# A decode kernel on one core: half of the last row of `wo` loaded early through three DMA engines, and exp on pairs of tiles

## The chip, the cores and the metric

The kernel runs on one core of a Trainium2 chip. The metric is the device time of one execution in microseconds (us), here the median of three to nine runs. The core has a tensor engine (PE, with a separate row PEld for its weight loads), a vector engine (DVE), a scalar engine (ACT), GpSimd (POOL), a sync engine (SP, which here only issues loads) and 16 DMA engines that move data from HBM into the on-chip memory (SBUF, 128 partitions).

## The reference, cut to what matters

One token passes through attention against a cache of 65,536 keys and values (32 query heads, 4 key/value heads), and through a gated MLP; a gate mixes the two.

```python
def _A_ref(x, k_cache, v_cache, wq, wo):        # x 1x1x1024, caches 1x4x65536x128, bf16
    q = (x @ wq) ...                            # wq 1024 x 4096
    scores = jnp.einsum('bhqd,bhkd->bhqk', q, k) * Dh ** (-0.5)
    p = _softmax(scores, axis=-1)
    o = jnp.einsum('bhqk,bhkd->bhqd', p, v)
    return o.reshape(B, Sq, Hq * Dh) @ wo       # wo 4096 x 1024
...
return g * a + (1 - g) * b                      # b: the MLP with w_in and w_out
```

The caches are 134 MB of the 162 MB that must be read. `wo` is the last thing needed, 8 MB.

## The kernel before: the parts that matter here

Everything large passes through one tile, `kv`, of five slots of 32 KB per partition. One function issues every load from the sync engine's queue.

```python
WO_SPLIT = ((16,), (8, 4, 2, 1, 1))
...
    const = ctx.enter_context(tc.tile_pool(name="const", bufs=1))
    wk = ctx.enter_context(tc.tile_pool(name="wk", bufs=2))
    big = ctx.enter_context(tc.tile_pool(name="big", bufs=1))     # kv lies behind const and wk
    scp = ctx.enter_context(tc.tile_pool(name="scp", bufs=NT + 1))
    ptp = ctx.enter_context(tc.tile_pool(name="ptp", bufs=NT + 2))
...
    kv = big.tile([P, NKV * CT * P], BF16, name="kv")
    def load(src, shape, at):
        ...
        v = kv[:, int(at * CT * P):int(at * CT * P) + n]
        ins = nc.sync.dma_start(out=v, in_=src)
```

Softmax works tile by tile, four tiles for each of the four key/value heads:

```python
        for j in range(NT):
            nc.scalar.activation(out=sct[g, j][:], in_=sct[g, j][:], func=ACT.Exp, scale=SCALE,
                                 bias=nb[:, 0:1], accum_out=lss[g][:, j:j + 1])
            ptt[g, j] = ptp.tile([P, CC, B], BF16, name="pt")
            nc.vector.transpose(out=ptt[g, j][:].rearrange("p c x -> p (c x)"),
                                in_=sct[g, j][:])
```

At the end, partition p holds rows 32p to 32p+31 of `wo`, and they arrive in pieces of 16, 8, 4, 2, 1 and 1 rows per partition, each multiplied as it comes. The pieces get smaller so that little work is left after the last one.

```python
    wo_view = A_wo.rearrange("(p c) n -> p c n", c=OC)            # OC = 32
    c0 = 0
    for at, split in enumerate(WO_SPLIT):
        for n in split:
            t = load(wo_view[:, c0:c0 + n, :], (n, D), at + c0 % (OC // 2) * D / (CT * P))
            project(t, n, oa, c0, last=(c0 + n == OC))
            c0 += n
    ...
    nc.scalar.copy(out=out_sb[:], in_=out_ps[:])                  # then two 1 KB output DMAs
```

## Time and profile before

| | before |
|---|---|
| time, median (lowest to highest) | 383.25 us (383.17 to 383.29) |
| span of the profile | 381.4 us |
| DMA engines busy, queue 1 | 98.7% of 16 engines' span |
| read from HBM | 162.01 MB, 425 GB/s over the span |
| PE, DVE, ACT busy | 61%, 57%, 10% |

The first lines are from the page: busy us and share of the span by engine; the DMA's busy tenths in 40 equal slices; then the DMA queues with packets, MB and share of 16 engines' time. Queue 1 carries the loads, queues 8 and 14 carry instructions for the engines themselves.

```profile
PE 232.4 (61%) x1372; PEld 56.8 (15%) x796; DVE 218.4 (57%) x211; ACT 39.6 (10%) x55; POOL 4.4 (1%) x10
...
DMA  9999999999999999999999999999999999999995
...
q1 hardware_dynamic: 4324, 162.01, 98.7%
q8 instruction: 8, 0.13, 0.1%
q14 instruction: 3, 0.02, 0.0%
```

The DMA engines are the limit: they are full in all slices but the last. What can be gained without moving fewer bytes is what lies in that last slice. The windows view shows it: each row is a stretch of time, and its last two columns are the DMA engines' busy share and GB/s.

```profile
core 0: us, PE busy (x) PEld busy (x) DVE busy (x) ACT busy (x) POOL busy (x), PEclk, DMA share, GB/s
371.20:376.00 4.80, 3.79 (x85) 2.87 (x77) 0.00 (x0) 0.00 (x0) 0.00 (x0) 0.70 0.98 398
376.00:377.00 1.00, 0.62 (x16) 0.42 (x16) 0.00 (x0) 0.00 (x0) 0.00 (x0) 1.00 0.83 322
377.00:378.00 1.00, 0.40 (x8) 0.28 (x8) 0.00 (x0) 0.00 (x0) 0.00 (x0) 0.75 0.58 215
378.00:379.00 1.00, 0.69 (x12) 0.19 (x7) 0.00 (x0) 0.00 (x0) 0.00 (x0) 0.50 0.08 29
```

The share falls in steps over 2 us, so the 16 engines do not finish together, though each has the same bytes to move. The timeline of the same end, and the softmax of one head group (start us, us, engine, line, operation, and in brackets the idle time before and what ended it):

```profile
377.60 1.08 PE L478 MATMUL out_ps<-kv,oa 128*32 128x256 bf16 x12 [0.64 <-DMA kv<-in_A_wo_dram]
378.92 0.41 PE L478 MATMUL out_ps<-kv,oa 128*32 128x256 bf16 x4 [0.24 <-DMA kv<-in_A_wo_dram]
379.37 0.37 ACT L521 CAST out_sb<-out_ps 128x256 bf16<-128x256 f32 x1 [45.36 <-PE out_ps L478]
379.77 0.32 SPq L524 DMA_DIRECT2D out_dram<-out_sb  x1
```

```profile
252.14 0.16 DVE L420 TENSOR_SCALAR nb<-nb_ps 128x1 f32<-128x1 f32 x1 [0.53 <-PE nb_ps L417]
253.66 4.64 DVE L427 STREAM_TRANSPOSE pt<-sc 128x1024 bf16<-128x1024 bf16 x4 [1.37 <-ACT sc L424]
...
275.76 0.33 SPq L167 DMA_DIRECT2D kv<-in_A_k_cache_dram  x1
```

The last matmuls wait for the last piece of `wo`, so the kernel ends when the slowest DMA engine ends. The load that SP issues at 275.76 joins a queue that is not empty: the load ahead of it finished at 279.1 to 281.1 on the 16 engines.

**Following single DMA engines.** The trace holds the start, length, size and queue of every DMA packet, though not its engine. An engine takes its next packet 3 or 4 ns before the previous record ends, so packets can be chained into 16 lanes, one for each engine (where two lanes coincide to the nanosecond their names can be swapped; ends and packet lengths are not affected). In the kernel before, seven lanes write their last completion at 376.31 to 377.09 us of the span and nine at 377.89 to 378.37. The late ones are those that an instruction fetch fell on: eight 16,384-byte packets of queue 8, one on each of eight engines, each of which sets its engine back by 1.55 us for the rest of the run, and two 8,192-byte packets of queue 14 that fell on a ninth. The third packet of queue 14, at 318 us, fell on one of the seven early lanes and sets it back by about 0.7 us; it is the one that ends at 377.09.

### The profile page before, as it was taken

What the parts mean: (1) busy time and instruction counts of PE and PEld (TensorE: products, weight loads), DVE (VectorE), ACT (ScalarE), POOL (GpSimd) and SP (SyncE); (2) the same over time, 40 slices, a digit from 0 to 9 for tenths busy, and PEclk for the clock granted to TensorE, in tenths of its full rate; (3) what the DMA queues carried; (4) which work ended last, traced back from release to release, by engine and by line L of the source; (5) the groups of instructions that cost most, each with busy time, mean ns of one, the idle gap of its engine ahead of it and who ended that gap; (6) DMA issues with size and microseconds to landing.
All of it is one profiled execution on the core that took longest, in us unless ns stands there. A gap on an engine that the chain in (4) does not pass through costs nothing.

```text
span 381.4 us, 2581 instructions
## 1 busy us (share of the span) xinstructions
PE 232.4 (61%) x1372; PEld 56.8 (15%) x796; DVE 218.4 (57%) x211; ACT 39.6 (10%) x55; POOL 4.4 (1%) x10
## 2 busy tenths in 40 slices
PE   0433467678157944796397629872967196849355
PEld 0110011112011210121011101120111011212123
DVE  4241487996687506966977059669780488550040
ACT  1010001111601100114010001050001010500000
POOL 4000000000000000000000000000000000000000
PEclk9966659998759895989588959895799679969766
DMA  9999999999999999999999999999999999999995
GB/s 376 439 426 416 433 436 440 436 461 429 400 426 440 440 435 426 440 440 440 440 428 440 440 440 433 428 427 406 433 440 428 426 433 427 440 411 436 440 405 230
DMA packets 4375, 162.17 MB, mean 425 GB/s; under 512 B 520, under 2 KB 524, under 8 KB 908
## 3 DMA queue, kind: packets, MB, share of 16 engines
q1 hardware_dynamic: 4324, 162.01, 98.7%
q8 instruction: 8, 0.13, 0.1%
q14 instruction: 3, 0.02, 0.0%
q10 hardware_dynamic: 40, 0.01, 0.0%
HBM read 162.01 MB, written 0.00 MB: 425 GB/s over the span
## 4 chain that ended last, share of the span: by engine, by line
DMA 59%; PE 20%; DVE 16%; issue 2%; ACT 1%; SPq 1%; DVEq 0%; ACTq 0%
DMA kv<-in_A_k_cache_dram 37%; PE s_ps L391 15%; DVE kv L384 9%; DMA kv<-in_A_wo_dram 8%; DMA kv<-in_A_wq_dram 7%; DMA kv<-in_A_v_cache_dram 7%; PE o_ps L437 3%; DVE pt L427 2%; DVE mx L386 1%; DVE o_sb L451 1%; PE q_ps L277 1%; ACT sc L424 1%; DVE rowt L447 1%; ACT sc L402 1%; SPq L167 1%
## 5 line engine op out<-in xcount | busy, mean ns | idle before, releaser
L391 PE MATMUL s_ps<-kv,wt 128*128 128x512 bf16 x512 | 142.1, 437 | 81.8 <-DVE kv L384 81.7
L384 DVE STREAM_TRANSPOSE kv<-kv 128x2048 int32<-128x2048 int32 x64 | 142.7, 2280 | 55.5 <-DMA kv<-in_A_k_cache_dram 55.5
L437 PE MATMUL o_ps<-kv,pt 128*64 128x512 bf16 x512 | 61.6, 399 | 7.7 <-DMA kv<-in_A_v_cache_dram 7.7
L391 PEld LDWEIGHTS <-wt 128*128 128x128 bf16 x256 | 27.5, 108 | 197.6 <-issue 140.2
L402 ACT CAST sc<-s_ps 128x1024 bf16<-128x1024 f32 x16 | 16.2, 1013 | 253.5 <-PE s_ps L391 253.5
L437 PEld LDWEIGHTS <-pt 128*64 128x64 bf16 x256 | 16.0, 115 | 50.7 <-issue 48.1
L427 DVE STREAM_TRANSPOSE pt<-sc 128x1024 bf16<-128x1024 bf16 x16 | 18.6, 1217 | 6.8 <-ACT sc L424 6.8
L386 DVE TENSOR_REDUCE mx<-sc 128x1 f32<-128x1024 bf16 x12 | 14.5, 1207 | 10.1 <-ACT sc L402 10.1
L424 ACT ACTIVATE sc<-sc,nb 128x1024 bf16<-128x1024 bf16 x16 | 18.2, 1137 | 12.2 <-DVE nb L420 12.2
L447 DVE TENSOR_TENSOR rowt<-o_ps,own 128x1024 f32<-128x1024 f32 x4 | 4.8, 1194 | 24.9 <-PE o_ps L437 24.9
L457 PE MATMUL om_ps<-o_sb,hsel 128*32 128x128 f32 x8 | 2.5, 421 | 19.7 <-DVE o_sb L451 19.7
L406 DVE TENSOR_REDUCE mx<-sc 128x1 f32<-128x1024 bf16 x4 | 4.9, 1220 | 14.2 <-ACT sc L402 14.2
L277 PE MATMUL q_ps<-kv,xT 128*32 128x512 bf16 x64 | 7.2, 627 | 7.4 <-DMA kv<-in_A_wq_dram 7.4
L478 PE MATMUL out_ps<-kv,oa 128*32 128x256 bf16 x128 | 6.7, 366 | 3.7 <-DMA kv<-in_A_wo_dram 2.2
L277 PE MATMUL z_ps<-kv,xT 128*32 128x448 bf16 x64 | 6.2, 570 | 3.8 <-DMA kv<-in_B_w_in_dram 3.8
L344 DVE TENSOR_TENSOR rowt<-q_ps,own_b 128x512 f32<-128x512 f32 x2 | 1.3, 686 | 12.5 <-PE q_ps L277 12.5
L451 DVE TENSOR_REDUCE o_sb<-rowt 128x128 f32<-128x1024 f32 x4 | 7.5, 1872 | 0.1
L292 DVE TENSOR_TENSOR rowt<-z_ps,own_b 128x448 f32<-128x448 f32 x2 | 1.2, 620 | 8.5 <-PE z_ps L277 8.5
L233 PE MATMUL xb_ps<-xg,spread 8*128 8x256 bf16 x1 | 0.4, 367 | 9.1 <-DMA xg<-in_gate_w_dram 9.1
L277 PEld LDWEIGHTS <-xT 128*32 128x32 bf16 x64 | 3.0, 139 | 19.4 <-issue 19.3
L478 PEld LDWEIGHTS <-oa 128*32 128x32 bf16 x128 | 4.4, 124 | 6.1 <-issue 3.3
L521 ACT CAST out_sb<-out_ps 128x256 bf16<-128x256 f32 x1 | 0.4, 372 | 45.4 <-PE out_ps L478 45.4
(88 smaller groups left out, 54.8 us busy)
## 6 DMA issues: line engine op xcount, KB each, us to landing
kv<-in_A_k_cache_dram SPq DMA_DIRECT2D x4, 4096.0 KB, 26.8
kv<-in_A_wq_dram SPq DMA_DIRECT2D x2, 4096.0 KB, 32.8
kv<-in_A_v_cache_dram SPq DMA_DIRECT2D x2, 4096.0 KB
kv<-in_B_w_in_dram SPq DMA_DIRECT2D x2, 3584.0 KB, 15.0
kv<-in_A_wo_dram SPq DMA_DIRECT2D x1, 4096.0 KB
kv<-in_B_w_out_dram SPq DMA_DIRECT2D x1, 3584.0 KB
kv<-in_A_wo_dram SPq DMA_DIRECT2D x1, 2048.0 KB, 28.6
kv<-in_A_wo_dram SPq DMA_DIRECT2D x1, 1024.0 KB, 30.7
```

The lines of the kernel that those rows point to most:

```text
L277: ins = nc.tensor.matmul(ps[t * B:(t + 1) * B, k * HN:k * HN + n], lhsT=xT[:, i * KH + c:i * KH + c + 1].to_broadcast([P, B]), rhs=w[:, c, ...
L384: nc.vector.transpose(out=kb[:, v * n:(v + 1) * n], in_=kb[:, v * n:(v + 1) * n])
L386: nc.vector.reduce_max(**late.pop())
L391: ins = nc.tensor.matmul(s_ps[:, k * HN:(k + 1) * HN], lhsT=wt[g % 2][:, v, b].rearrange("p a v h -> p (a v h)"), rhs=kx[:, b // 2, b % 2, ...
L402: nc.scalar.copy(out=sct[g, j][:], in_=s_ps[:])
L406: nc.vector.reduce_max(**late.pop())
L424: nc.scalar.activation(out=sct[g, j][:], in_=sct[g, j][:], func=ACT.Exp, scale=SCALE, bias=nb[:, 0:1], accum_out=lss[g][:, j:j + 1])
L427: nc.vector.transpose(out=ptt[g, j][:].rearrange("p c x -> p (c x)"), in_=sct[g, j][:])
L437: ins = nc.tensor.matmul(o_ps[g][hs, e, :], lhsT=ptt[g, j][:, 2 * u:2 * u + 2, :].rearrange("p c x -> p (c x)"), rhs=vx[:, 2 * u + e], sta ...
L447: nc.vector.tensor_tensor(out=om8, in0=o_ps[g][:].rearrange("p e (v d) -> p (e v) d", d=DH), in1=own_8[:].unsqueeze(2).to_broadcast([P, 2 ...
L451: nc.vector.tensor_reduce(out=o_sb[:], in_=om8.rearrange("p x d -> p d x"), axis=AX.X, op=ALU.add)
L478: nc.tensor.matmul(out_ps[t * B:(t + 1) * B, :], lhsT=vec[:, c0 + c:c0 + c + 1].to_broadcast([P, B]), rhs=w[:, c, t * NO:(t + 1) * NO], st ...
```

## The change

Its intent is to even out that end. The last row of each partition is 256 KB. For the 64 even partitions it is still loaded last, by all 16 engines. For the 64 odd ones it is loaded early, between the loads of the caches, in seven small loads of nine rows and one of one row. Each of the seven has an outer dimension of 3 and is meant for three engines that finish early. The rows land in a tile `moved` on partitions 0 to 23, three rows each, and a one-hot matmul brings the matching attention outputs there. To make room in SBUF, exp and the transposes that follow run on pairs of tiles with fewer buffers. Eight dummy matmuls, two groups of 1.04 us in the trace, keep PE busy around the last head's output.

```diff
-WO_SPLIT = ((16,), (8, 4, 2, 1, 1))
+WO_SPLIT = ((16,), (8, 4, 2, 1))
+MA, MB, MM = 3, 8, 3
-    scp = ctx.enter_context(tc.tile_pool(name="scp", bufs=NT + 1))
-    ptp = ctx.enter_context(tc.tile_pool(name="ptp", bufs=NT + 2))
+    scp = ctx.enter_context(tc.tile_pool(name="scp", bufs=NT // 2))
+    ptp = ctx.enter_context(tc.tile_pool(name="ptp", bufs=NT // 2 + 1))
+    moved = const.tile([MA * MB, MM, D], BF16, name="moved")
+    src_row = const.tile([P, MM, MA, MB], FP32, name="src_row")
... (one-hot tables; some small tiles go from double to single buffers)
-        for j in range(NT):
-            nc.scalar.activation(out=sct[g, j][:], in_=sct[g, j][:], func=ACT.Exp, scale=SCALE,
-                                 bias=nb[:, 0:1], accum_out=lss[g][:, j:j + 1])
+        for h in range(NT // 2):
+            sc = sct[g, h][:].rearrange("p t x -> p (t x)")
+            nc.scalar.activation(out=sc, in_=sc, func=ACT.Exp, scale=SCALE,
+                                 bias=nb[:, 0:1], accum_out=lss[g][:, h:h + 1])
+            ptt[g, h] = ptp.tile([P, 2 * CC, B], BF16, name="pt")
+            nc.vector.transpose(out=ptt[g, h][:].rearrange("p c x -> p (c x)"), in_=sc)
...
+    last_odd = wo_view[1::2, OC - 1, :]
+    def load_moved(b):
+        r0, na, nm = b * MA * MM, MA, MM          # the eighth load: one row
+        ...
+        nc.sync.dma_start(
+            out=moved[b:b + (na - 1) * MB + 1:MB, :nm, :],
+            in_=last_odd[r0:r0 + na * nm, :].rearrange("(a m) d -> a m d", m=nm))
...
             vn = load_kv(A_v_cache, g - 1, 2 * h, 3, 2)
+            load_moved(2 * g - 2 + h)
...
+    keep_busy(4)
     head_out(G - 1)
+    keep_busy(4)
...
+    t = kv[:, c0 * D:(c0 + 1) * D]
+    nc.sync.dma_start(out=t[0::2, :], in_=wo_view[0::2, c0, :])
+    project(t.unsqueeze(1), 1, oa_kept, 0, last=True)
```

The new tiles stand in the pool ahead of `kv`, so `kv` moves from byte 28128 of each partition to byte 30784.

More of the change, by code (lines that the diff above doesn't have):

```diff
@@ L64 @@
     assert S % (P * CT) == 0 and F == 2 * NB * ZN and ZN == B * FC and HD == NHB * NB * HN
-    assert NHB * NB == 2 * G and CC * B == 2 * HN and sum(map(sum, WO_SPLIT)) == OC
+    assert NHB * NB == 2 * G and CC * B == 2 * HN and sum(map(sum, WO_SPLIT)) == OC - 1
     const = ctx.enter_context(tc.tile_pool(name="const", bufs=1))
@@ L203 @@
     nc.gpsimd.memset(ones_f[:], 1.0)
+    moved = const.tile([MA * MB, MM, D], BF16, name="moved")
+    nc.gpsimd.memset(moved[:], 0.0)
+    src_row = const.tile([P, MM, MA, MB], FP32, name="src_row")
+    nc.gpsimd.iota(src_row[:], pattern=[[2, MM], [2 * MM, MA], [2 * MM * MA, MB]], base=1,
+                   channel_multiplier=0, allow_small_or_imprecise_dtypes=True)
     wt = [big.tile([P, VC, BP, NB, VC, REP], BF16, name=f"wt{i}") for i in range(2)]
@@ L206 @@
         nc.gpsimd.memset(t[:], 0.0)
-    pbits = const.tile([P, 6], I32, name="pbits")
+    pbits = const.tile([P, 7], I32, name="pbits")
     for i, m in enumerate((P // KC - 1, B - 1, QD - 1, REP - 1)):
@@ L215 @@
                             scalar2=2 * VC - 1, op0=ALU.logical_shift_right, op1=ALU.bitwise_and)
-    pf = const.tile([P, 7], FP32, name="pf")
+    nc.vector.tensor_scalar(out=pbits[:, 6:7], in0=pidx[:], scalar1=1, scalar2=None,
+                            op0=ALU.bitwise_and)
+    pf = const.tile([P, 8], FP32, name="pf")
     nc.vector.tensor_copy(out=pf[:, 0:1], in_=pidx[:])
-    nc.vector.tensor_copy(out=pf[:, 1:7], in_=pbits[:])
+    nc.vector.tensor_copy(out=pf[:, 1:8], in_=pbits[:])
     def one_hot(shape, dtype, in0, col, name):
@@ L234 @@
                      start=True, stop=True)
-    xm = const.tile([P, 2, KC, P // KC], FP32, name="xm")
+    rowt = big.tile([P, 2 * HN], FP32, name="rowt")
+    xm = rowt[:, :2 * P].rearrange("p (t c i) -> p t c i", t=2, c=KC)
     for t in range(2):
@@ L240 @@
     xa = const.tile([P, 2, KC], FP32, name="xa")
-    nc.vector.tensor_reduce(out=xa[:], in_=xm[:], axis=AX.X, op=ALU.add)
+    nc.vector.tensor_reduce(out=xa[:], in_=xm, axis=AX.X, op=ALU.add)
     xT = const.tile([P, KC], BF16, name="xT")
@@ L267 @@
     own_q = one_hot([P, QD], FP32, row[:, :QD], 3, "own_q")
+    move = one_hot([P, MM * MA * MB], BF16, src_row[:].rearrange("p m a b -> p (m a b)"), 0, "move")
+    keep = const.tile([P, 1], BF16, name="keep")
+    nc.vector.tensor_scalar(out=keep[:], in0=pf[:, 7:8], scalar1=-1.0, scalar2=1.0, op0=ALU.mult,
+                            op1=ALU.add)
     hsel = one_hot([P, REP, QD], FP32, row[:, :REP].unsqueeze(2).to_broadcast([P, REP, QD]), 4,
@@ L287 @@
         x_rows(z_ps, win_t[i], ZN, i)
-    rowt = big.tile([P, 2 * HN], FP32, name="rowt")
     om8 = rowt[:].rearrange("p (x d) -> p x d", d=DH)
@@ L400, in k_tile @@
             mxs[g] = wk.tile([P, NT], FP32, name="mx")
-        sct[g, j] = scp.tile([P, CC * B], BF16, name="sc")
-        nc.scalar.copy(out=sct[g, j][:], in_=s_ps[:])
-        late.append(dict(out=mxs[g][:, j:j + 1], in_=sct[g, j][:], axis=AX.X))
+        if (g, j // 2) not in sct:
+            sct[g, j // 2] = scp.tile([P, 2, CC * B], BF16, name="sc")
+        sc = sct[g, j // 2][:, j % 2]
+        nc.scalar.copy(out=sc, in_=s_ps[:])
+        late.append(dict(out=mxs[g][:, j:j + 1], in_=sc, axis=AX.X))
     def stats(g):
@@ L413, in stats @@
                                 axis=AX.X, op=ALU.max)
-        gr = wk.tile([1, P // REP, REP], FP32, name="gr")
+        gr = big.tile([1, P // REP, REP], FP32, name="gr")
         nc.vector.tensor_copy(out=gr[:], in_=gm[:].unsqueeze(1).to_broadcast([1, P // REP, REP]))
@@ L421, in stats @@
                                 op0=ALU.mult)
-        lss[g] = wk.tile([P, NT], FP32, name="ls")
-        for j in range(NT):
-            nc.scalar.activation(out=sct[g, j][:], in_=sct[g, j][:], func=ACT.Exp, scale=SCALE,
-                                 bias=nb[:, 0:1], accum_out=lss[g][:, j:j + 1])
-            ptt[g, j] = ptp.tile([P, CC, B], BF16, name="pt")
-            nc.vector.transpose(out=ptt[g, j][:].rearrange("p c x -> p (c x)"),
-                                in_=sct[g, j][:])
+        lss[g] = wk.tile([P, NT // 2], FP32, name="ls")
+        for h in range(NT // 2):
[4 more added lines that the diff above has]
+            nc.vector.transpose(out=ptt[g, h][:].rearrange("p c x -> p (c x)"), in_=sc)
     def v_tile(g, j, vt):
@@ L435, in v_tile @@
             hs = slice(u % 2 * P // 2, (u % 2 + 1) * P // 2)
+            c0 = j % 2 * CC + 2 * u
             for e in range(2):
@@ L438, in v_tile @@
                     o_ps[g][hs, e, :],
-                    lhsT=ptt[g, j][:, 2 * u:2 * u + 2, :].rearrange("p c x -> p (c x)"),
+                    lhsT=ptt[g, j // 2][:, c0:c0 + 2, :].rearrange("p c x -> p (c x)"),
                     rhs=vx[:, 2 * u + e], start=(j == 0 and u < 2),
@@ L449, in head_out @@
             in1=own_8[:].unsqueeze(2).to_broadcast([P, 2 * VC, DH]), op=ALU.mult)
-        o_sb = wk.tile([P, DH], FP32, name="o_sb")
+        o_sb = big.tile([P, DH], FP32, name="o_sb")
         nc.vector.tensor_reduce(out=o_sb[:], in_=om8.rearrange("p x d -> p d x"), axis=AX.X,
                                 op=ALU.add)
-        om_ps = psm.tile([P, DH + NT], FP32, name="om_ps", tag="m")
+        om_ps = psm.tile([P, DH + NT // 2], FP32, name="om_ps", tag="m")
         hs = hsel[:].rearrange("p h q -> p (h q)")
@@ L461, in head_out @@
         nc.vector.reciprocal(out=rl[gs, 1:2], in_=rl[gs, 0:1])
-        om = wk.tile([P, QD, OC], FP32, name="om")
+        om = big.tile([P, QD, OC], FP32, name="om")
         nc.vector.tensor_tensor(
@@ L470, in head_out, with keep_busy @@
                                 scalar2=gate[gs, :], op0=ALU.mult, op1=ALU.mult)
+    def keep_busy(n):
+        ps = pss.tile([P, 2 * HN], FP32, name="busy_ps", tag="s")
+        w = wt[G % 2][:].rearrange("p v b t u h -> p (v b t u h)")
+        for i in range(n):
+            ins = nc.tensor.matmul(ps[:, :HN], lhsT=w[:, :P], rhs=w[:, :HN], start=True,
+                                   stop=True, skip_group_check=True)
+            if i > 0:
+                same_weights(ins)
     NO = D // NB
@@ L479, in project @@
                     out_ps[t * B:(t + 1) * B, :],
-                    lhsT=vec[:, c0 + c:c0 + c + 1].to_broadcast([P, B]),
+                    lhsT=vec[:, c0 + c:c0 + c + 1].to_broadcast([vec.shape[0], B]),
                     rhs=w[:, c, t * NO:(t + 1) * NO],
@@ L483, in project @@
                     skip_group_check=True)
+    wo_view = A_wo.rearrange("(p c) n -> p c n", c=OC)
+    last_odd = wo_view[1::2, OC - 1, :]
+    def load_moved(b):
+        r0, na, nm = b * MA * MM, MA, MM
+        if r0 + MA * MM > P // 2:
+            assert r0 == P // 2 - 1
+            na, nm = 1, 1
+        nc.sync.dma_start(
+            out=moved[b:b + (na - 1) * MB + 1:MB, :nm, :],
+            in_=last_odd[r0:r0 + na * nm, :].rearrange("(a m) d -> a m d", m=nm))
     build_w(0)
@@ L506 @@
     for j, n, at in ((0, 2, 1), (2, 1, 3), (3, 1, 4)):
-        for i, vt in enumerate(load_kv(A_v_cache, G - 1, j, at, n)):
+        vn = load_kv(A_v_cache, G - 1, j, at, n)
+        if j < 3:
+            load_moved(MB - 2 + j // 2)
+        for i, vt in enumerate(vn):
             v_tile(G - 1, j + i, vt)
+    keep_busy(4)
     head_out(G - 1)
-    wo_view = A_wo.rearrange("(p c) n -> p c n", c=OC)
+    keep_busy(4)
     c0 = 0
@@ L516 @@
             t = load(wo_view[:, c0:c0 + n, :], (n, D), at + c0 % (OC // 2) * D / (CT * P))
-            project(t, n, oa, c0, last=(c0 + n == OC))
+            project(t, n, oa, c0)
             c0 += n
+            if c0 == OC // 2:
+                mv_ps = psm.tile([MA * MB, MM], FP32, name="mv_ps", tag="m")
+                for m in range(MM):
+                    nc.tensor.matmul(mv_ps[:, m:m + 1],
+                                     lhsT=move[:, m * MA * MB:(m + 1) * MA * MB],
+                                     rhs=oa[:, OC - 1:OC], start=True, stop=True,
+                                     skip_group_check=True)
+                oa_moved = wk.tile([MA * MB, MM], BF16, name="oa_moved")
+                nc.vector.tensor_copy(out=oa_moved[:], in_=mv_ps[:])
+                oa_kept = wk.tile([P, 1], BF16, name="oa_kept")
+                nc.vector.tensor_tensor(out=oa_kept[:], in0=keep[:], in1=oa[:, OC - 1:OC],
+                                        op=ALU.mult)
+            if c0 == OC - OC // 4:
+                project(moved, MM, oa_moved, 0)
+    t = kv[:, c0 * D:(c0 + 1) * D]
+    nc.sync.dma_start(out=t[0::2, :], in_=wo_view[0::2, c0, :])
+    project(t.unsqueeze(1), 1, oa_kept, 0, last=True)
     out_sb = const.tile([P, NO], BF16, name="out_sb")
```

## The prediction

> **What bounds the kernel.** The 16 DMA engines. In the 40-slice view DMA is 9 tenths in 39 slices; queue 1 fills 98.7% of 16 engines' span, 162.01 MB at 425 GB/s. PE (61%) and DVE (57%) hide beneath it. Loads are issued 4 us or more before the previous load's last packet has landed (sync engine's timeline beside the packets' completion writes), so the engines do not run dry. In the windows at the end the DMA share falls 0.98, 0.83, 0.58, 0.08 (371-376, then each us to 379): the engines do not finish together. Following each engine's packets in the trace, seven end 1.2 to 2.1 us before the last one, nine within 0.5 us of it. The late ones are those that once served a 16,384-byte packet of the instruction queue (eight, 1.02 to 1.10 us each), which puts that engine's later completions back 1.55 us for good. [...]
>
> **What the change does.** The bytes stay. The last row per partition (256 KB, eight 2,048-byte packets per engine, 84 ns each, one every 81 ns) becomes four packets per engine: 4 x 81 ns = 0.32 us less on every engine. The other 64 rows go early to few engines[...]. Each gets 21 rows, 21 x 81 ns = 1.7 us (estimate). So the change pays if those three are early ones: they would end level with the late ones (-1.9 + 1.7). [...]
>
> Moved besides:
> - exp on pairs: first exp about 2.1 us in place of 1.14, so the transposes of pt end about 0.8 us later per head group, and loads are issued up to 0.8 us later; the 4 us lead covers that. It mainly makes room for `moved`.
> - eight busy matmuls (0.4 us each) around the last head's output, while PE waits anyway (3.1 and 1.4 us).
> - twelve matmuls for `moved` (0.6 us) before the 4-column piece, whose data comes at 376.3; the first 24 columns were done at 375.0. Off the path.
> - a few tiny operations and eight small DMA issues, about 0.4 us each of an idle sequencer.
>
> **On the path:** only the end of the wo stream: last landing 378.9 to about 378.6; then the same tail (matmuls 0.43, cast 0.37, output DMA).
>
> **Prediction:** 383.22 - 0.3 = 382.95 us, 8 in 10 between 382.6 and 383.8. Faster by over 2% 0.005, within 2% 0.985, slower by over 2% 0.01.
>
> **What would show it right:** the last project begins about 0.3 us earlier; the spread of the engines' last packets is smaller; loads still lead, slices still 9; transposes of pt about 0.8 us later per group; instruction refills still eight.
>
> **What would make it wrong:** if one of the three engines has served a refill, it ends 1.7 - 0.3 = 1.4 us after the end of before: about 384.6 us. If refills fall on other engines from run to run, the times scatter by that. If 2 KB packets between K and V cost more than 81 ns, part of the gain goes. If the late exp makes loads late, a slice under 9 shows it. If `moved`'s matmuls delay the last pieces, the gain is given back there.

383.22 us less about 0.3 us for the shorter end of the stream gives the 382.95 us (382.92 by the rounded figures). "Those three" are the three engines that I took an outer dimension of 3 to use. No trace of the kernel before showed it; that of the changed kernel has the early rows on three lanes.

## More of the kernel before

Each of the three groups of experiments ran on another chip, with the kernel before beside it (medians 383.28, 383.25 and 383.20 us), so times of different groups can be compared to about 0.1 us.

## The result, and the profile after

| | before | after |
|---|---|---|
| time, median (lowest to highest), 5 runs | 383.25 us (383.17 to 383.29) | 383.58 us (383.50 to 383.88) |
| span of the profile | 381.4 us | 381.6 us |
| last completion write of the loads, us of the span | 378.37 | 378.60 |
| time minus span | 1.8 to 1.9 us | 1.9 to 2.4 us |

The ratio of after to before is 1.0012, with a 95% interval from 0.9998 to 1.0025. A ratio here is the mean time of one kernel's runs over that of the other's of the same rounds, so it is not quite the ratio of the medians quoted. The interval is about 1 us wide in all, which is more than most effects; so the verdicts below rest on the traces, and on the spans of all runs, as much as on the times.

The same views of the changed kernel: the page's lines, the windows of the end, the timeline of the end, and the softmax of the same head group with the same load.

```profile
PE 229.6 (60%) x1395; PEld 56.0 (15%) x813; DVE 221.1 (58%) x208; ACT 37.3 (10%) x39; POOL 7.2 (2%) x12
...
DMA  9999999999999999999999999999999999999995
...
q1 hardware_dynamic: 4346, 162.01, 98.8%
q8 instruction: 8, 0.13, 0.1%
q14 instruction: 2, 0.02, 0.0%
```

```profile
371.20:376.00 4.80, 3.47 (x111) 2.94 (x112) 0.32 (x3) 0.00 (x0) 0.00 (x0) 1.00 0.97 399
376.00:377.00 1.00, 0.02 (x4) 0.02 (x7) 0.00 (x0) 0.00 (x0) 0.00 (x0) 1.00 0.87 342
377.00:378.00 1.00, 0.60 (x16) 0.40 (x16) 0.00 (x0) 0.00 (x0) 0.00 (x0) 1.00 0.72 277
378.00:379.00 1.00, 0.54 (x12) 0.30 (x12) 0.00 (x0) 0.00 (x0) 0.00 (x0) 1.00 0.11 39
```

```profile
378.86 0.29 PE L502 MATMUL out_ps<-kv,oa 128*32 128x256 bf16 x4 [0.22 <-DMA kv<-in_A_wo_dram]
379.15 0.41 PE L502 MATMUL out_ps<-kv,oa_kept 128*32 128x256 bf16 x4
379.60 0.37 ACT L579 CAST out_sb<-out_ps 128x256 bf16<-128x256 f32 x1 [45.65 <-PE out_ps L502]
380.00 0.28 SPq L582 DMA_DIRECT2D out_dram<-out_sb  x1
```

```profile
251.07 0.16 DVE L434 TENSOR_SCALAR nb<-nb_ps 128x1 f32<-128x1 f32 x1 [0.53 <-PE nb_ps L431]
253.45 4.50 DVE L442 STREAM_TRANSPOSE pt<-sc 128x2048 bf16<-128x2048 bf16 x2 [2.22 <-ACT sc L439]
...
274.68 0.34 SPq L168 DMA_DIRECT2D kv<-in_A_k_cache_dram  x1
```

The end is more even than before (0.72 in place of 0.58 in the third row of the windows), as intended, but the whole of it comes later: the last project begins at 379.15 and not at 378.92. The pairs of exp act as predicted: from `nb` to the end of the transposes of `pt` it takes 253.45 + 4.50 - 251.07 = 6.9 us, against 253.66 + 4.64 - 252.14 = 6.2 us before. No load is late for it: SP issues the same load at 274.68, even earlier than before, while the load ahead of it ends at 279.0 to 281.2, and from 12 us to the `wo` pieces no engine pauses for over 0.1 us but at instruction fetches.

The chains of packets show that three points of the plan work. The nine rows of an early load lie on three lanes, three each, so the load does run on three engines. These three lanes serve no instruction fetch. And the half row shortens the end of every lane: from the last completion but one to the last it takes 0.67 us on the earliest lane before, 0.34 us after.

But the chains also show packets that have grown. In the kernel before, a packet of 65,536 bytes takes 2,419 to 2,428 ns, and only those beside an instruction fetch take more. Here is what the changed kernel's trace has around the sixth early load (start in ns of the span, length in ns, bytes, cut to the packets over 9 ns):

```
317501 2698 65536
317770 2536 65536
...
319197   84  2048
319204   84  2048
319272 2533 65536
319274 2532 65536
319277   84  2048
...
319451 2614 65536
319564 2532 65536
319650 2689 65536
319679 2532 65536
319715 2571 65536
```

Here every lane's packet that is in flight just after the early load takes some 110 ns more, and a few take 250 ns more. This happens at early loads 4, 5 and 6 (counted from 0), with most packets longer by some 80 ns at load 4, 110 at load 5 and 130 at load 6, where they have 32,768 bytes. At loads 0 to 3 only one to three lanes are hit.

### The profile page after: what moved, and what is told of

It reads as the page before. It is cut to its first block, busy times and chain, and to the rows that moved or that the text cites. A ratio compares the mean times of both kernels' runs of the same rounds, so it can differ in the third digit from the quotient of the medians. Undisturbed runs are those within 1.5% of the kernel's fastest.

```text
span 381.6 us, 2611 instructions
## 1 busy us (share of the span) xinstructions
PE 229.6 (60%) x1395; PEld 56.0 (15%) x813; DVE 221.1 (58%) x208; ACT 37.3 (10%) x39; POOL 7.2 (2%) x12
## 4 chain that ended last, share of the span: by engine, by line
DMA 59%; PE 19%; DVE 17%; issue 2%; ACT 2%; SPq 0%; DVEq 0%; ACTq 0%
DMA kv<-in_A_k_cache_dram 37%; PE s_ps L403 14%; DVE kv L396 10%; DMA kv<-in_A_wo_dram 8%; DMA kv<-in_A_wq_dram 7%; DMA kv<-in_A_v_cache_dram 7%; PE o_ps L452 3%; DVE pt L442 2%; DVE mx L398 2%; ACT sc L439 1%; DVE o_sb L466 1%; PE q_ps L290 1%; DVE rowt L462 1%; ACT sc L416 1%; SPq L168 0%
## 5 line engine op out<-in xcount | busy, mean ns | idle before, releaser
L403 PE MATMUL s_ps<-kv,wt 128*128 128x512 bf16 x512 | 138.0, 426 | 84.3 <-DVE kv L396 84.1
L452 PE MATMUL o_ps<-kv,pt 128*64 128x512 bf16 x512 | 62.5, 403 | 6.7 <-DMA kv<-in_A_v_cache_dram 6.7
L442 DVE STREAM_TRANSPOSE pt<-sc 128x2048 bf16<-128x2048 bf16 x8 | 18.0, 2290 | 10.2 <-ACT sc L439 10.2
L439 ACT ACTIVATE sc<-sc,nb 128x2048 bf16<-128x2048 bf16 x8 | 15.9, 1994 | 12.2 <-DVE nb L434 12.2
L502 PE MATMUL out_ps<-kv,oa 128*32 128x256 bf16 x124 | 4.3, 274 | 3.5 <-DMA kv<-in_A_wo_dram 3.1
L226 DVE CAST pf<-pbits 128x7 f32<-128x7 int32 x1 | 6.1, 6099 | 0.0
L230 DVE TENSOR_SCALAR spread<-erow,pf 8x128 bf16<-8x128 f32 x1 | 6.0, 6011 | 0.0
```

Source lines behind the costliest of these rows:

```text
L226: nc.vector.tensor_copy(out=pf[:, 1:8], in_=pbits[:])
L230: nc.vector.tensor_scalar(out=t[:], in0=in0, scalar1=pf[:shape[0], col:col + 1], scalar2=None, op0=ALU.is_equal)
L403: ins = nc.tensor.matmul(s_ps[:, k * HN:(k + 1) * HN], lhsT=wt[g % 2][:, v, b].rearrange("p a v h -> p (a v h)"), rhs=kx[:, b // 2, b % 2, ...
L439: nc.scalar.activation(out=sc, in_=sc, func=ACT.Exp, scale=SCALE, bias=nb[:, 0:1], accum_out=lss[g][:, h:h + 1])
L442: nc.vector.transpose(out=ptt[g, h][:].rearrange("p c x -> p (c x)"), in_=sc)
L452: ins = nc.tensor.matmul(o_ps[g][hs, e, :], lhsT=ptt[g, j // 2][:, c0:c0 + 2, :].rearrange("p c x -> p (c x)"), rhs=vx[:, 2 * u + e], star ...
```

## The experiments

Theories at the start of the experiments:

- **P, partitions.** An early load takes more than its own packets' time, and how much depends on the partitions that it writes. Early load b of the changed kernel writes partitions b, b+8 and b+16: loads 0 to 3 write 0-3, 8-11 and 16-19, loads 4 to 6 write 4-6, 12-14 and 20-22. The border lies just where the trace has it, between loads 3 and 4. I supposed a cause behind this, which would make some partitions free of the cost (`own_port`) and others dear (`all_foreign`). No trace here shows that cause, and the two names stand only for the sets of partitions that these runs write.
- **H, HBM.** What disturbs is the reading of rows that lie 128 KB apart.
- **E, engines.** Pairs of exp or busy matmuls make loads late.

Two more theories, A and F, came from the runs.

### First four: no early loads, two other sets of partitions, near rows

`no_moved` takes the calls of `load_moved` away (wrong result; the tolerance did not notice).

```diff
-            load_moved(2 * g - 2 + h)
...
-        if j < 3:
-            load_moved(MB - 2 + j // 2)
```

> The changed kernel without the eight early loads; `moved` stays zero, so the result is wrong on purpose. All else of the change stays (pairs of exp, busy matmuls, half row at the end). Theory P (the early loads take more from the 16 DMA engines than their packets[...]): no 65,536-byte packet over 2,440 ns but the eight that follow an instruction refill; the last landing 0.3 us before that of the kernel before; about 382.9 us. Rival E (pairs of exp or busy matmuls make the loads late): stays near 383.5 us.

Measured: 383.01 us (382.78 to 383.36), ratio 0.9994, interval 0.9981 to 1.0006. The last completion is at 377.93 us, 0.44 us ahead of the kernel before. No packet of 65,536 bytes exceeds 2,440 ns but those beside an instruction fetch. So the half row pays at the end of the stream, pairs of exp and busy matmuls cost nothing there, and the early loads cost 378.60 - 377.93 = 0.67 us. Rival E falls.

`own_port` loads the same rows to other partitions: load b writes b, b+4 and b+8 for b of 0 to 3, so 0-11 in all, and loads 4 to 6 write 32-34, 36-38 and 40-42:

```diff
-    moved = const.tile([MA * MB, MM, D], BF16, name="moved")
+    moved = const.tile([MP, MM, D], BF16, name="moved")         # MP = 64
-    src_row = const.tile([P, MM, MA, MB], FP32, name="src_row")
+    src_row = rowt[:, HN:HN + MM * MP]                          # did not fit otherwise
...
+        p0 = 32 * (b // 4) + b % 4
-            out=moved[b:b + (na - 1) * MB + 1:MB, :nm, :],
+            out=moved[p0:p0 + (na - 1) * 4 + 1:4, :nm, :],
```

> The changed kernel with the same 22 early rows per engine, but [...] (0-3 and 32-35, 4-7 and 36-39, 8-11 and 40-43), in place of 0-23. Right result. Theory P: the slow packets after the early loads (up to 2,698 ns against 2,420) are gone, the three engines fall back by about 250 ns per load and not 330 to 360, and the time is about 382.9 us. Rival H (small reads far apart in HBM are what disturbs) and rival E: stays near 383.5 us.

Measured: 382.39 us (382.34 to 382.98), ratio 0.998, interval 0.9967 to 0.9993. That is better than theory P allowed (382.9 us), and a reason to distrust it.

`all_foreign` gives each early load the pattern of loads 4 to 6, on partitions 4-7, 12-15 and 20-23 (loads 0 to 3) and those plus 32 (the rest):

```diff
+        p0 = 32 * (b // 4) + b % 4 + 4
+            out=moved[p0:p0 + (na - 1) * 8 + 1:8, :nm, :],
```

> The changed kernel with every early load written in the pattern of its loads 4 to 6: [...] (4-7, 12-15, 20-23 and those plus 32). Right result. Theory P: all seven loads, not three, hold up every engine by about 0.1 us each, so some 0.4 us more: about 383.9 us. Rivals H and E: as the changed kernel, 383.6 us.

Measured: 382.99 us (382.75 to 383.23), ratio 0.9995. By the time alone this contradicts P: it should have been slower than the changed kernel and is 0.6 us faster. Yet its trace has 81 packets of 65,536 bytes over 2,440 ns away from any fetch, where the changed kernel has 43. Something else had sped it up.

`near_rows` reads nine rows that lie together, to the same partitions (wrong result, again unnoticed):

```diff
-            in_=last_odd[r0:r0 + na * nm, :].rearrange("(a m) d -> a m d", m=nm))
+            in_=A_wo[r0:r0 + na * nm, :].rearrange("(a m) d -> a m d", m=nm))
```

> The changed kernel with the early loads reading nine rows that lie together in HBM in place of rows 128 KB apart; same partitions written; wrong result on purpose. Theory P: as the changed kernel, 383.6 us, with the same slow packets around the loads. Rival H: the slow packets are gone and the time is about 383.0 us.

Measured: 383.64 us (383.33 to 384.12), ratio 1.0011, with the same long packets at the same loads. Rival H falls: it is not where the rows lie in HBM.

What `own_port` and `all_foreign` share is that a table was moved out of the pool ahead of `kv` to make room, so that `kv` starts at byte 30720, a multiple of 512, and not at 30784. In both traces nearly every 65,536-byte packet takes exactly 2,418 ns; in the changed kernel the middle half take 2,420 to 2,427, in the kernel before 2,421 to 2,426. That is **theory A, address**: where `kv` starts sets the length of the packets that are written to it. My first four runs had mixed two things, and the next four separate them.

### Second four: address and partitions apart

`before_aligned` is the kernel before with one unused tile ahead of `kv`, and nothing else (the tile moves every tile behind it by 544 bytes, not `kv` alone):

```diff
+    pad = const.tile([P, 136], FP32, name="pad")      # kv at 28672 in place of 28128
```

> The kernel before with 544 unused bytes per partition ahead of `kv`, so that `kv` starts at byte 28672 of each partition (a multiple of 512) and not at 28128 (32 past a multiple of 64). Nothing else. Theory A (the two layouts of the own_port and all_foreign runs were fast because `kv` began at 30720 there): every 65,536-byte packet takes 2,418 ns (2,419 to 2,428 before), which over the stream is 0.8 us per engine: about 382.5 us. If it is not the address: 383.25 us.

Measured: 381.75 us (381.68 to 381.94), ratio 0.9961, interval 0.9947 to 0.9975. Theory A holds, and gives more than I expected: the packets take 2,418 ns, the last completion is at 377.23 (378.37 before), and from that to the last project takes 0.35 us in place of 0.55. Part of the surplus can be read in the lanes: a 16,384-byte instruction fetch sets its engine back by 1.42 to 1.43 us here, and not by 1.55. That the address acts through `kv`, and not through another tile that moved with it, is taken from the packets, nearly all of which are written to `kv`. The span and the end of its timeline:

```profile
span 380.0 us, 2581 instructions
...
376.98 0.29 PE L480 MATMUL out_ps<-kv,oa 128*32 128x256 bf16 x4 [0.24 <-DMA kv<-in_A_wo_dram]
377.58 0.29 PE L480 MATMUL out_ps<-kv,oa 128*32 128x256 bf16 x4 [0.30 <-DMA kv<-in_A_wo_dram]
377.92 0.37 ACT L523 CAST out_sb<-out_ps 128x256 bf16<-128x256 f32 x1 [45.17 <-PE out_ps L480]
```

The same instructions run, 2,581 of them, and the last project begins at 377.58, 1.34 us earlier than in the kernel before.

`after_aligned` is the changed kernel with `kv` at 30720 and its early loads as they were:

```diff
+    pad = const.tile([P, 56], FP32, name="pad")
-    src_row = const.tile([P, MM, MA, MB], FP32, name="src_row")
+    src_row = rowt[:, HN:HN + MM * MA * MB]
```

> The changed kernel, early loads to its own partitions 0-23, but `kv` at byte 30720 in place of 30784 (a table moved into `rowt`, 224 bytes of padding). Theories A and P together: packets of 2,418 ns, so 0.65 us less than the changed kernel, 382.95 us, with the slow packets after the early loads still there; 0.5 us behind own_port. Without A: 383.6 us. Without P: 382.4 us, as own_port.

Measured: 382.50 us (382.19 to 382.97), ratio 0.9981, interval 0.9968 to 0.9993. The address is worth 1.1 us to the changed kernel, more than I expected. By the time alone this is the number that I had expected without P (382.4 us). But the long packets are still there (36 away from fetches, `own_port` has 3), and the last completions of the three destinations with `kv` at 30720 stand in the order that P demands: 377.17 us in `own_port`, 377.38 in `after_aligned`, 378.08 in `all_foreign`. In the aligned layout the early loads of the changed kernel cost only the 0.2 us between the first two.

`own_port_off` and `all_foreign_off` are the earlier two with 64 unused bytes, so that `kv` is at 30784 as in the changed kernel:

```diff
+    pad = const.tile([P, 16], FP32, name="pad")
```

> own_port with 64 unused bytes ahead of `kv`, so that it starts at 30784 as in the changed kernel. [...] Theory P: no slow packets after the loads, about 383.0 us. Without P (all of own_port's gain was the address): 383.5 us.

> all_foreign with `kv` at 30784 as in the changed kernel. Theory P: all seven loads slow many engines, so it is no faster than the changed kernel: 383.6 to 384.0 us. Without P: 383.5 us or less.

Measured: 382.97 us (382.63 to 383.24), ratio 0.9991, interval 0.9979 to 1.0004; and 384.51 us (384.37 to 384.68), ratio 1.0032, interval 1.0019 to 1.0046. With the address held, the three destinations stand in the order that P demands, 382.97, 383.58 and 384.51, and the last is worse than I dared to expect. The intervals of the first two overlap, but the spans of all their runs do not: 380.6 to 381.0 us in `own_port_off`, 381.4 to 381.6 in the changed kernel, 382.4 in `all_foreign_off`. The cost can be read from a lane that no fetch and no early load touches. What its packets take beyond the normal length, added up over packets that are more than 40 ns too long:

| kernel (`kv` at 30784 but in before) | long packets of such a lane | together | last completion, us | time, us |
|---|---|---|---|---|
| before (`kv` at 28128) | 0 | 0 | 378.37 | 383.25 |
| no_moved | 0 | 0 | 377.93 | 383.01 |
| own_port_off | 0 | 0 | 377.78 | 382.97 |
| after | 3 | 343 ns | 378.60 | 383.58 |
| near_rows | 3 | 422 ns | 378.51 | 383.64 |
| all_foreign_off | 7 | 836 ns | 379.41 | 384.51 |

One long packet for each load that writes partitions 4-7, 12-15 and 20-23 or those plus 32: none, three, seven. Writing the partitions of `own_port_off` takes the cost of the early loads away: it ends no later than `no_moved` (its spans are 380.6 to 381.0 us, those of `no_moved` 380.7 to 381.1). Six of its packets away from fetches do exceed 2,440 ns, all between 95 and 100 us, before its first early load moves at 124 us; what made them is not known. Around the sixth load, where the changed kernel's packets took 2,532 ns and more, `own_port_off` has this:

```
318966   84  2048
319046   85  2048
319056   84  2048
319116   84  2048
319125 2418 65536
...
319213 2418 65536
319302 2418 65536
319364 2418 65536
319405 2418 65536
```

Why loads 4 to 6 hold up every engine, while loads 0 to 3 (partitions 0-3, 8-11 and 16-19) hold up a few, is not shown. Shown is that the destination makes the cost, and that the partitions of `own_port_off` avoid it. What sets these partitions apart from the others is not shown: no run wrote further sets, and no trace names the engine or the partitions of a packet.

One thing remained: 382.97 for `own_port_off` is still little better than `no_moved` and only 0.3 us better than before, though its last completion is 0.59 us ahead of before. The missing part lies outside the span.

### Last four: exp, and the loose ends

In every run of the kernel before (and of `before_aligned`, which has its program), time minus span is 1.8 to 1.9 us. In kernels with pairs of exp it is 1.9 to 2.0 in some runs and 2.2 to 2.5 in others. Among their profiled runs, four have a late 8,192-byte packet of queue 14 after the end of the loads, and those four have 2.26, 2.28, 2.44 and 2.48 us; the others, which show no such packet, have at most 2.0. The queues of `own_port` from 370 us to the end:

```profile
q1 hardware_dynamic: 567, 2.54, 47.4%
q8 instruction: 1, 0.02, 0.5%
q14 instruction: 1, 0.01, 0.2%
```

In the kernel before, three packets of 8,192 bytes are seen during the loads (50, 256 and 318 us); in the changed kernel two (31 and 258 us). **Theory F, fetch**: pairs of exp shorten an instruction stream (the pages count 39 instructions of ACT in place of 55, 208 of DVE in place of 211), so one fetch that fell into the run now falls behind its end and lengthens the time there.

`single_exp` puts exp and the transposes back on single tiles, in the pair buffers:

```diff
+            for i in range(2):
+                sc = sct[g, h][:, i]
+                nc.scalar.activation(out=sc, in_=sc, func=ACT.Exp, scale=SCALE,
+                                     bias=nb[:, 0:1], accum_out=lss[g][:, j:j + 1])   # j = 2h+i
+                nc.vector.transpose(... ptt[g, h][:, i * CC:(i + 1) * CC] ..., in_=sc)
```

> The changed kernel with exp and the transposes of pt tile by tile again, in the same pair buffers; `kv` at 30784 as in the changed kernel. Theory F (the pairs leave the scalar engine some 19 instructions fewer, so that its last 8,192-byte instruction fetch falls behind the kernel's end, where in about half of the runs it adds 0.4 us outside the span): an 8,192-byte packet before the end of the stream as in the kernel before, time minus span steady at 1.8 to 1.9 us in all runs (1.9 to 2.4 in the changed kernel), 383.4 us. Rival E (the pairs make loads late): the span itself is shorter by 0.3 us or more.

Measured: 383.73 us (383.67 to 383.96), ratio 1.0015, interval 1.0001 to 1.0028. The fetch is back in the run (at 334 us), and time minus span is 1.82 to 1.88 in all five runs. So far F holds. But the span is longer, 381.8 to 382.1, not shorter: rival E has nothing here. The lane that ends last, at 378.90 us, is one of the three with early rows, and it is the lane on which the returned fetch fell. The queues from 370 us to the end, now without queue 14:

```profile
q1 hardware_dynamic: 601, 3.10, 58.1%
q8 instruction: 1, 0.02, 0.5%
q10 hardware_dynamic: 4, 0.00, 0.0%
```

`own_port_single` joins the partitions of `own_port`, the aligned `kv` and single exp:

> The best guess: [...]`kv` at 30720, exp tile by tile. If theories A, P and F add up: span 380.0 us as own_port, time minus span 1.85 us, 381.8 us, level with before_aligned (381.75), so the early loads bring less than 0.2 us net even then. If the early loads bring their full 0.3 us: 381.45 us.

Measured: 382.46 us (382.23 to 382.67), ratio 0.998, interval 0.9967 to 0.9992: a miss. Time minus span is steady (1.83 to 1.88), but the span grew to 380.4 to 380.8. The reason is seen in the profiled run: the fetch at 333.7 us fell on a lane with early rows, which ends at 377.89 us while the next ends at 377.19. The gain outside the span was lost inside.

`before_128` asks how round the address must be:

```diff
+    pad = const.tile([P, 40], FP32, name="pad")       # kv at 28288 = 221 * 128
```

> The kernel before with 160 unused bytes, so that `kv` starts at 28288, a multiple of 128 and not of 256. If a start at a multiple of 128 is enough for the 2,418 ns packets: 381.75 us as before_aligned. If it takes 256 or 512: packets of 2,418 to 2,428 ns, 383.0 to 383.25 us.

Measured: 382.90 us (382.82 to 382.99), ratio 0.9992, interval 0.9978 to 1.0005; the middle half of the packets take 2,419 to 2,424 ns. A multiple of 128 is not enough. Whether 256, 512 or 1024 is was not run: both fast addresses (28672 and 30720) are multiples of 2048.

`no_busy` takes the dummy matmuls out:

```diff
-    keep_busy(4)
     head_out(G - 1)
-    keep_busy(4)
```

> The changed kernel without the eight busy matmuls. All theories: as the changed kernel, 383.6 us, because the project matmuls wait for data[...].

Measured: 383.61 us (383.40 to 384.05), ratio 1.0012, as the changed kernel. They bring nothing and cost nothing.

The fastest version is the kernel before with `kv` moved by 544 bytes, 381.75 us. No version with early loads beat it. In `own_port`, the best of them, the lane that ends last is one of the three with early rows, and its last completion at 377.17 us is only 0.06 us ahead of that in `before_aligned` (377.23): once the address is right, the change has next to nothing left to gain.

## Why the prediction was right or wrong

The range held (382.6 to 383.8, measured 383.58), but the gain of 0.3 us that it was built on was not there, and the kernel became 0.33 us slower by the medians. That the range held says little for the reasoning: it was wide enough to hold the kernel before as well. Point by point:

- **What bounds the kernel: right.** The DMA engines, and of these the slowest at the end. Instruction fetches of 16,384 bytes set engines back by 1.55 us each; the changed kernel's trace has eight of them as well.
- **The half row saves 0.32 us on every engine: right.** 0.67 to 0.34 us between the last two completions.
- **Three engines, 1.7 us each, none of them one with a fetch: right.** That the loads would use three engines was not shown by any trace before; the changed kernel's trace shows three lanes (it does not name the engines). A load of three rows holds its engine for 245 to 253 ns, seven times that is 1.7 us.
- **Pairs of exp 0.8 us later per head group, covered by the lead: right** (0.7 us), and no load was late.
- **"On the path: only the end of the wo stream: last landing 378.9 to about 378.6": this step failed.** It took an early row to cost only the engine that moves it. Early loads 4 to 6, which write partitions 4-6, 12-14 and 20-22, hold up every engine, by some 80 to 130 ns a load. By `no_moved`, the early loads cost 0.67 us of the last completion, against a gain of 0.44 us without them. The lane that ends last in the changed kernel, at 378.60, is not one of the three. It is the lane with two 8,192-byte fetches, which ends last in `no_moved` too, and loads 4 to 6 lengthened four of its packets by 179, 278, 128 and 147 ns, together 0.73 us. My list of what could go wrong had slow 2 KB packets, and a fetch on one of the three engines; it did not have harm to the others.
- **What was not looked at, first: the address of `kv`.** The new tiles shift it by 2,656 bytes. By luck this cost nothing: a lane's many small excesses over 2,418 ns (and over the shortest length of the smaller packets) sum to 0.8 us before and 0.65 us after, which fits the 0.44 that `no_moved` gained in place of 0.33. At either address the kernel pays over 1 us for it.
- **Second: the instructions that pairs of exp remove.** They let a fetch slip behind the end, which adds about 0.4 us outside the span in some of the runs (two of the five of the changed kernel: 383.78 and 383.88). I took pairs of exp for a matter of buffers. Which engine's stream it is was not separated: pairs shorten both the scalar engine's (55 to 39 instructions on the pages) and the vector engine's (211 to 208).

## What to carry to other kernels

When the DMA engines are the limit, follow single packets: a length that differs by 0.2% over the whole stream, or steps of 100 ns at a few loads, can cost more than evening out a tail of 0.3 us brings. Put the tile that all loads land in at a round address (here two multiples of 2048 bytes did it; multiples of 32, 64 and 128 did not: packets of 2,418 ns against mostly 2,419 to 2,428), and check the address again after adding any tile ahead of it. Try small loads on a few engines with other destination partitions: on a lane that carried none of them, the same rows cost 836 ns in `all_foreign_off`, 343 ns in the changed kernel and nothing in `own_port_off`. And a change of the number of instructions can move a fetch onto the engine that has no slack (the one at 334 us in `single_exp`), or behind the end (`own_port`).
